# Local attention of a head pair: from three blocks of three query tiles to one block of nine

## Chip, cores and metric

One core of one Trainium2 chip runs the whole program. The metric is the device time of one execution in microseconds (us); for the kernel before it is 1076.56 us, the median of three runs (1076.06 to 1077.1).

## What is computed

An attention with 2 batches, 8 heads, 576 positions and a head width of 64 feeds a layer with 8 experts and then a dense layer with a softplus. The change touches the attention alone, which adds two parts: a coarse attention over means of 4 positions, and a local one in which a position sees only positions less than 4 away. All is fp32.

```python
def _attn_ref(q, k, v):
    ...
    out_d = sm_attn(q_d, k_d, v_d)              # means of 4 positions
    out_up = np.repeat(out_d, factor, axis=2)
    mask = np.abs(pos[:, None] - pos[None, :]) < factor
    scores = scale * np.matmul(q, k.transpose(0, 1, 3, 2))
    scores = np.where(mask, scores, -1000000000.0)
    scores = scores - np.max(scores, axis=-1, keepdims=True)
    attn = np.exp(scores)
    attn = attn / (np.sum(attn, axis=-1, keepdims=True) + 1e-09)
    out_local = np.matmul(attn, v)
    return (out_up + out_local).astype(np.float32)
```

## The kernel before

**Units.** The attention is cut into eight units, one for each pair of heads: units 0 to 3 are batch 0, units 4 to 7 batch 1. A unit has 9 query tiles of 64 positions. A local query tile meets a window of 72 keys. `load` fetches q, k and v of a unit; there is one buffer for q and k (`qk`), so the load of a unit waits until the unit before has been transposed. `setup(g)` transposes three tiles into the bank `tb`, from which VectorE (DVE) sums groups of 4 (L535), ScalarE (ACT) scales the keys (L546), and both copy the queries into `fine`, in which the columns of one head are zero in the rows of the other (L547, L548).

**Blocks.** A unit then goes through four blocks: `c`, the coarse part, and 0, 1 and 2, three query tiles each, with both heads side by side in the 128 rows. Each block has three steps. `scores` forms the products into one PSUM bank `sc` (for a local block one product lays the mask there at L572 and three add the scores at L578), takes the maximum of each row (DVE, L585), three exponentials with their sums (ACT, L590), the reciprocal and the product with it (DVE, L591 to L593). `turn` transposes the result (L615) and ACT copies it (L616). `values` multiplies by v (L637), and DVE adds the coarse part into `xf` (L652).

**Order.** The loop at L1039 walks 32 blocks and issues `scores` of block n, `turn` of block n-2 and `values` of block n-3; `setup` of the next unit stands beside blocks 1 and 2. A scheduler then orders the instructions of each engine, and each engine works through its list in that order. `stir` (L481) issues products that nothing reads, in units 0 to 3 only.

**Beside the attention.** Once the four units of batch 0 are done, `operands` turns their output into the split operands of the expert products (subtractions at L437, rounding on ACT at L439, remainders on DVE at L441). The first four steps of the expert products (L841, L929) run among the units of batch 1. When the last unit is done, the operands of the other tokens are formed, and the rest of the program follows in an order fixed by a planner; its instructions are not touched by the change.

Of the kernel before, what the change touches and what calls it, by code (L numbers as in the profile page):

```python
# [9 lines left out]
F32 = mybir.dt.float32  # L10
F32R = mybir.dt.float32r
U32 = mybir.dt.uint32
BF16 = mybir.dt.bfloat16
# [7 lines left out]
def attention_moe_mlp(ctx: ExitStack, tc: tile.TileContext, q, k, v, w_gate, w1, w2, w_in, w_out, out):  # L21
# [10 lines left out]
    NQ = S // QT  # L32
    NB = 3
# [30 lines left out]
    ps = ctx.enter_context(tc.tile_pool(name="ps", bufs=1, space=PSUM))  # L64

    def bank(tag, name):
# [394 lines left out]
    mask = ap.tile([P, NB + 2, KW], BF16, bufs=1, name="mask")  # L461
    nc.gpsimd.memset(mask, 0.0)
    for t0, t1, off in ((0, 1, 0), (1, NB + 1, R), (NB + 1, NB + 2, 2 * R)):

        for hh in range(2):
            part = mask[hh * QT : (hh + 1) * QT, t0:t1, :]
            for sign in (1, -1):
                nc.gpsimd.affine_select(
                    out=part, in_=part, compare_op=ALU.is_gt, fill=NEG,
                    base=R + sign * off, pattern=[[0, t1 - t0], [-sign, KW]], channel_multiplier=sign,  # L470
                )
    rest = const.tile([P, KD, LEFT], F32, name="rest")

    fine = [ap.tile([P, NB, 2, QT], F32, bufs=1, name=f"fine{g}") for g in range(NB)]
    flat = [ap.tile([P, NB, 2, CT], F32, bufs=1, name=f"flat{i}") for i in range(2)]
    for x in fine + flat:
        nc.gpsimd.memset(x, 0.0)
# [8 lines left out]
    class Unit:  # L486
# [9 lines left out]
        def bank(self, name, kind):  # L496
            return bank(("m", "at", "y")[kind] if self.b == 0 else "at", name)
# [23 lines left out]
        def setup(self, g):  # L521

            if g == 0:
                self.kT = ap.tile([P, NQ, QT], F32, tag="kT", name="kT")
# [4 lines left out]
            for j in range(NB):  # L529
# [4 lines left out]
            tbv = tb.rearrange("x (t w p) -> x t w p", t=NB, w=2)  # L534
# [23 lines left out]
        def scores(self, blk):  # L558

            sc = self.bank("sc", 0)  # L560
            stir(sc, 1 if self.n < 4 else 0)
            if blk == "c":
                rows, w = 2 * CT, SD
                for i in range(NB):
                    nc.tensor.matmul(
                        sc[:rows, i * w : (i + 1) * w], self.flat[:, i].rearrange("x h q -> x (h q)"),
# [616 lines left out]
```

## Time and profile before

| what | us |
|---|---|
| three runs | 1076.06, 1076.56, 1077.1 |
| median | 1076.56 |
| span of the profiled execution | 1075.4 |
| last value products of the attention | 140.8 to 141.7 |

The span goes from the first to the last instruction. The profiled execution has no time listed beside its span; the median of the runs lies 1.16 us above it. In the views, PE is TensorE's product stream and PEld its weight load, DVE is VectorE, ACT ScalarE, POOL GpSimd, SP the engine that issues the transfers. A product in fp32 leaves two records, a transpose one. PEclk is the clock granted to TensorE as a share of 2.4 GHz; 0.50 is 1.2 GHz.

### The profile page before, as it was taken

What the parts mean: (1) busy time and instruction counts of PE and PEld (TensorE: products, weight loads), DVE (VectorE), ACT (ScalarE), POOL (GpSimd) and SP (SyncE); (2) the same over time, 40 slices, a digit from 0 to 9 for tenths busy, and PEclk for the clock granted to TensorE, in tenths of its full rate; (3) what the DMA queues carried; (4) which work ended last, traced back from release to release, by engine and by line L of the source; (5) the groups of instructions that cost most, each with busy time, mean ns of one, the idle gap of its engine ahead of it and who ended that gap; (6) DMA issues with size and microseconds to landing.
All of it is one profiled execution on the core that took longest, in us unless ns stands there. A gap on an engine that the chain in (4) does not pass through costs nothing.

```text
span 1075.4 us, 17729 instructions
## 1 busy us (share of the span) xinstructions
PE 1052.5 (98%) x6426; PEld 933.1 (87%) x6426; DVE 697.6 (65%) x1430; ACT 567.0 (53%) x1475; POOL 555.4 (52%) x575
## 2 busy tenths in 40 slices
PE   7989999999999999999999999999999999999998
PEld 4778888898989999898989989899998999788987
DVE  4797655776556566665656566565664678776765
ACT  3777634444444444454544444444454667676663
POOL 4556614477566566655566565664575412232221
PEclk8989989999999999999999999999999999999999
DMA  7654301222433334243333333343324373253112
GB/s 156 128 137 92 92 1 40 59 87 78 138 108 98 113 93 127 92 130 108 118 122 95 93 95 112 98 124 116 119 93 144 137 297 145 108 220 143 69 40 89
DMA packets 133495, 119.69 MB, mean 111 GB/s; under 512 B 35744, under 2 KB 111776, under 8 KB 133408
## 3 DMA queue, kind: packets, MB, share of 16 engines
q1 hardware_dynamic: 133408, 118.56, 36.1%
q8 instruction: 50, 0.82, 0.3%
q14 instruction: 37, 0.30, 0.1%
HBM read 93.11 MB, written 25.43 MB: 110 GB/s over the span
## 4 chain that ended last, share of the span: by engine, by line
PE 81%; DVE 10%; ACT 5%; POOL 1%; issue 1%; DMA 1%; SPq 1%; ACTq 0%; DVEq 0%
PE yps L929 40%; PE m L841 36%; DVE xl L441 2%; DVE ab L808 2%; POOL ab L805 1%; DVE ab L801 1%; ACT one L803 1%; PE sc L578 1%; DVE one L799 1%; ACT sc L590 1%; DVE c L860 1%; PE pv L637 1%; DVE hl L812 1%; PE tp L615 0%; DVE hl L780 0%
## 5 line engine op out<-in xcount | busy, mean ns | idle before, releaser
L841 PE MATMUL m<-xh,w1h 128*128 128x320 f32 (+1 forms) x1120 | 334.7, 299 | 2.8 <-DVE hl L780 1.6
L841 PE MATMUL m<-xl,w1h 128*128 128x320 f32 (+1 forms) x1120 | 333.3, 298 | 0.3 <-DVE xl L441 0.2
L841 PE MATMUL m<-xh,w1l 128*128 128x320 f32 (+1 forms) x1120 | 333.3, 298 | 0.0
L841 PEld LDWEIGHTS m<-xh,w1h 128*128 128x128 f32 x1120 | 213.1, 190 | 19.8 <-ACT t L853 2.8
L841 PEld LDWEIGHTS m<-xl,w1h 128*128 128x128 f32 x1120 | 213.1, 190 | 13.2 <-DVE xl L441 0.7
L841 PEld LDWEIGHTS m<-xh,w1l 128*128 128x128 f32 x1120 | 213.0, 190 | 0.4 <-POOL sums L244 0.2
L929 PE MATMUL yps<-w2h,hh 128*128 128x512 f32 x502 | 199.0, 396 | 2.2 <-ACT hh L810 2.2
L929 PE MATMUL yps<-w2l,hh 128*128 128x512 f32 x502 | 198.1, 395 | 0.0
L929 PE MATMUL yps<-w2h,hl 128*128 128x512 f32 x502 | 195.9, 390 | 0.0
L929 PE MATMUL yps<-w2h,h 128*128 128x512 f32 x436 | 153.0, 392 | 0.1
L295 POOL TENSOR_TENSOR w1l<-sums,w1h 128x512 fp32r<-128x512 f32 x72 | 99.2, 1389 | 88.7 <-ACT w1h L293 78.0
L860 DVE TENSOR_TENSOR c<-m,t 128x256 f32<-128x256 f32 (+1 forms) x160 | 72.7, 455 | 110.3 <-PE m L841 64.8
L316 POOL TENSOR_TENSOR w2l<-raw,w2h 128x512 fp32r<-128x512 f32 x72 | 98.4, 1385 | 59.8 <-ACT w2h L314 59.4
L805 POOL TENSOR_TENSOR ab<-one,ab 128x320 f32<-128x320 f32 (+1 forms) x64 | 54.6, 855 | 143.3 <-ACT one L803 143.3
L778 ACT ACTIVATE hh<-c 128x256 fp32r<-128x256 f32 (+1 forms) x138 | 61.0, 445 | 126.4 <-DVE c L860 126.2
L959 DVE SCALAR_TENSOR_TENSOR acc<-yps,pr,acc 128x512 f32<-128x512 f32 x117 | 87.3, 746 | 55.4 <-PE yps L929 54.7
L780 DVE SCALAR_TENSOR_TENSOR hl<-c,hh 128x256 fp32r<-128x256 f32 (+1 forms) x138 | 94.3, 687 | 33.0 <-ACT hh L778 31.4
L929 PEld LDWEIGHTS yps<-w2h,hl 128*128 128x128 f32 x502 | 94.3, 188 | 22.0 <-DVE hl L812 0.2
L929 PEld LDWEIGHTS yps<-w2h,hh 128*128 128x128 f32 x502 | 94.7, 189 | 15.2 <-ACT hh L810 2.6
L853 ACT COPY t<-m 128x256 f32<-128x256 f32 (+1 forms) x160 | 63.4, 398 | 78.4 <-PE m L841 78.2
L929 PEld LDWEIGHTS yps<-w2l,hh 128*128 128x128 f32 x502 | 94.8, 189 | 10.8
L929 PEld LDWEIGHTS yps<-w2h,h 128*128 128x128 f32 x436 | 82.0, 188 | 15.2 <-ACT h L810 0.3
(140 smaller groups left out, 1660.4 us busy)
## 6 DMA issues: line engine op xcount, KB each, us to landing
raw<-in_moe_w SPq DMA_DIRECT2D x72, 256.0 KB
raw<-in_moe_w SPq DMA_DIRECT2D x36, 512.0 KB
w1h<-s_in SPq DMA_DIRECT2D x10, 896.0 KB
w1l<-s_in SPq DMA_DIRECT2D x10, 896.0 KB
raw<-in_moe_w_in SPq DMA_DIRECT2D x32, 256.0 KB
raw<-in_moe_w_out SPq DMA_DIRECT2D x16, 512.0 KB
w2l<-s_out SPq DMA_DIRECT2D x10, 512.0 KB
w2h<-s_out SPq DMA_DIRECT2D x10, 512.0 KB
```

The lines of the kernel that those rows point to most:

```text
L295: behind(chain, nc.gpsimd.tensor_tensor(lo[:, part], sums, hi[:, part].bitcast(F32), op=ALU.subtract))
L316: behind(chain, nc.gpsimd.tensor_tensor(lo[:, i], raw[:, i], hi[:, i].bitcast(F32), op=ALU.subtract))
L441: nc.vector.tensor_tensor(xl[s][:, i, kk], src, xh[s][:, i, kk].bitcast(F32), op=ALU.subtract)
L778: nc.scalar.activation(hh, c, AF.Relu)
L780: nc.vector.scalar_tensor_tensor(out=hl, in0=c, scalar=0.0, in1=hh.bitcast(F32), op0=ALU.max, op1=ALU.subtract)
L805: nc.gpsimd.tensor_tensor(ab, one, ab, op=ALU.subtract)
L808: nc.vector.scalar_tensor_tensor(out=ab, in0=c, scalar=0.0, in1=ab, op0=ALU.max, op1=ALU.add)
L841: nc.tensor.matmul(b[:, :h], x[:, i, kk, :], y[s][:, i, kk, :], start=(not more and n == 0), stop=(n == 5), skip_group_check=more,)
L853: nc.scalar.copy(t, b[:, :h])
L860: nc.vector.tensor_tensor(c, b[:, :h], t, op=ALU.add)
L929: nc.tensor.matmul(y, a[:, f, tok], b[:, f, :], start=(start and m == 0), stop=(stop and m == 5))
L959: nc.vector.scalar_tensor_tensor(out=acc[t], in0=y, scalar=pr[:, t, e : e + 1], in1=acc[t], op0=ALU.mult, op1=ALU.add,)
```

## The change

The three local blocks of a unit become one block of nine tiles. Its scores lie in two PSUM banks (`two`), one for each head, five windows of 72 columns in each, with even tiles in rows 0 to 63 and odd tiles in rows 64 to 127. A product now has 64 rows of contraction and 64 of output, so `fine` and its zeros go; the keys are not scaled, ACT's exponential scales instead. DVE subtracts the maximum, one exponential on ACT covers all 720 columns, and DVE sums the rows. PSUM is dealt out anew: in batch 1 the single banks of the attention come from two buffers (`one`) where there were four (`at`). A copy of `rest` moves from DVE to ACT, and the values of a unit go through two banks (5 and 4 tiles) where there were three.

```diff
     def bank(tag, name):
...
-        return ps.tile([P, 512], F32, tag=tag, bufs=4 if tag == "at" else 1, name=name)
+        if tag in ("at", "one"):
+            return four[0].tile([P, 512], F32, tag=tag, bufs=4 if tag == "at" else 2, name=name)
+        return ps.tile([P, 512], F32, tag=tag, name=name)
...
-            return bank(("m", "at", "y")[kind] if self.b == 0 else "at", name)
+            return bank(("m", "one", "y")[kind] if self.b == 0 else "one", name)
...
+            nc.scalar.copy(
+                self.qkT[:, :, tiles].rearrange("x w t p -> x t w p"), tb.rearrange("x (t w p) -> x t w p", t=NB, w=2)
+            )
...
-            nc.scalar.mul(self.kT[:, tiles], tbv[:, :, 1], SCALE)
-            nc.vector.tensor_copy(fine[g][:D, :, 0], tbv[:D, :, 0])
-            nc.scalar.copy(fine[g][D:, :, 1], tbv[D:, :, 0])
...
+        def local(self):
+
+            sc = four[0].tile([P, 2, 512], F32, tag="two", name="sc2")
+            stir(sc[:, 0], 1 if self.n < 4 else 0)
+            kT = self.qkT[:, 1].rearrange("x t q -> x (t q)")
+            for hh in range(2):
+                nc.tensor.matmul(
+                    sc[:, hh, : NP2 * KW], identb, mask.rearrange("p t w -> p (t w)"),
+                    start=True, stop=False, skip_group_check=True,
+                )
+            for t in range(NQ):
+                w0 = min(max(t * QT - R, 0), S - KW)
+                for hh in range(2):
+                    half = slice(hh * D, (hh + 1) * D)
+                    nc.tensor.matmul(
+                        sc[t % 2 * QT : (t % 2 + 1) * QT, hh, t // 2 * KW : (t // 2 + 1) * KW],
+                        self.qkT[half, 0, t], kT[half, w0 : w0 + KW],
+                        start=False, stop=(t >= NQ - 2), skip_group_check=True,
+                    )
+            scv = sc[:, :, : NP2 * KW].rearrange("p h (i s) -> p h i s", i=NP2)
+            small = ap.tile([P, 3, 2, NP2, 1], F32, tag="smalls", name="smalls")
+            top, total, rs = [small[:, i] for i in range(3)]
+            ex = ap.tile([P, 2, NP2, KW], F32, tag="exl", bufs=1, name="exl")
+            whole = [P, 2, NP2, KW]
+            nc.vector.tensor_reduce(top, scv, axis=AX.X, op=ALU.max)
+            nc.vector.tensor_tensor(scv, scv, top.to_broadcast(whole), op=ALU.subtract)
+            nc.scalar.activation(scv, scv, AF.Exp, scale=SCALE)
+            nc.vector.tensor_reduce(total, scv, axis=AX.X, op=ALU.add)
+            nc.vector.tensor_scalar(rs, total, EPS, None, op0=ALU.add)
+            nc.vector.reciprocal(rs, rs)
+            nc.vector.tensor_tensor(ex, scv, rs.to_broadcast(whole), op=ALU.mult)
+            self.state["l"] = ex
...
-                et = ap.tile([KW, NB * P], F32, tag="et", name="et")
-                tp = self.bank("tp", 1)
-                stir(tp, 1 if self.n < 4 else 0)
-                for i in range(NB):
-                    nc.tensor.transpose(tp[:KW, i * P : (i + 1) * P], ex[:, i, :], ident)
-                nc.scalar.copy(et, tp[:KW, : NB * P])
+                et = ap.tile([KW, 2, S], F32, tag="et", bufs=1, name="et")
+                full = NQ // 2
+                for hh in range(2):
+                    tp = self.bank("tp", 0)
+                    stir(tp, 1 if self.n < 4 else 0)
+                    for i in range(full):
+                        nc.tensor.transpose(tp[:KW, i * P : (i + 1) * P], ex[:, hh, i], ident)
+                    nc.scalar.copy(et[:, hh, : full * P], tp[:KW, : full * P])
...
-    blocks = ["c", 0, 1, 2]
+    blocks = ["c", "l", None, None]
```

DVE's list for unit 2, before: L585 is a block's maximum, L591 to L593 its end, L535 a setup sum of unit 3, L652 an addition of unit 1 into `xf`.

```order
L585 TENSOR_REDUCE small<-sc 96x3
L585 TENSOR_REDUCE small<-sc 128x3
L652 TENSOR_TENSOR xf<-pv,xc 128x192
L585 TENSOR_REDUCE small<-sc 128x3
L535 TENSOR_REDUCE qkd<-tb 128x96 x2
L591 TENSOR_SCALAR small<-sc 96x3
L652 TENSOR_TENSOR xf<-pv,xc 128x192
L592 RECIPROCAL small<-small 96x3
L591 TENSOR_SCALAR small<-sc 128x3
L593 TENSOR_TENSOR ex<-sc,small 96x432
```

The same place with the change: L580 and L586 to L588 are the coarse block, L615, L616, L618 to L621 the local one, L537 the setup sums, L687 the additions into `xf`.

```order
L615 TENSOR_REDUCE smalls<-sc_527 128x10
L586 TENSOR_SCALAR small<-sc 96x3
L537 TENSOR_REDUCE qkd<-tb 128x96 x2
L616 TENSOR_TENSOR sc_527<-sc_527,smalls 128x2x360
L587 RECIPROCAL small<-small 96x3
L687 TENSOR_TENSOR xf<-pv,xc 128x256
L537 TENSOR_REDUCE qkd<-tb 128x96
L588 TENSOR_TENSOR exc<-sc,small 96x432
L694 COPY rest<-xf 128x64
L618 TENSOR_REDUCE smalls<-sc_527 128x10
L546 TENSOR_SCALAR flat_141<-qkd 64x3x48 x2
L619 TENSOR_SCALAR smalls<-smalls 128x10
```

L620 and L621 follow. Before, three maxima and three ends of blocks stand interleaved; now one chain of maximum, subtraction, sum and product runs through the list.

PE's list from the end of unit 1 into unit 2, before: a transpose group (L615), the mask and scores of one local block (L572, L578), the coarse scores (L565), value products of the block before (L637).

```order
L615 MATMUL tp<-ident,ex 72x128 x3
L481 LDWEIGHTS identb
L481 MATMUL sc<-identb 128x512
L572 LDWEIGHTS identb
L572 MATMUL sc<-mask,identb 128x216
L578 MATMUL sc<-kT,fine_149 128x72 x3
L565 MATMUL sc<-qkd,flat_152 96x144 x3
L637 MATMUL pv<-et,vw 64x64 x6
L615 MATMUL tp<-ident,ex 72x128 x3
```

With the change, from the transposes of unit 1's block (L645) to the last local scores of unit 2 (L605), L597 being the mask, L660 and L573 the coarse values and scores, L676 the value products:

```order
L645 MATMUL tp<-ident,exl 72x128 x8
L484 LDWEIGHTS identb
L484 MATMUL sc_527<-identb 128x512
...
L649 MATMUL tp<-ident,exl 72x64 x2
L660 MATMUL pv<-etc,vs 64x144 x3
L605 MATMUL sc_527<-qkT 64x72 x3
L484 LDWEIGHTS identb
L484 MATMUL sc<-identb 128x512
L573 MATMUL sc<-qkd,flat_140 96x144 x3
L605 MATMUL sc_527<-qkT 64x72 x8
L676 MATMUL pv<-et,vw 64x64 x10
L605 MATMUL sc_527<-qkT 64x72 x4
```

All scores of a unit now stand behind the transposes of the block before and partly behind its value products, where before a third of them did.

## Rows read from the trace of the kernel before

**Rows 1.** The page's first part: busy time of each engine over the span.

```profile
PE 1052.5 (98%) x6426; PEld 933.1 (87%) x6426; DVE 697.6 (65%) x1430; ACT 567.0 (53%) x1475; POOL 555.4 (52%) x575
```

**Rows 2.** Busy time by stretch: PE, PEld, DVE, ACT, POOL, granted clock, DMA.

```profile
28.00:58.00 30.00, 25.42 (x268) 19.74 (x263) 23.59 (x81) 23.51 (x107) 16.27 (x20) 1.00 0.61 134
58.00:68.00 10.00, 10.00 (x45) 7.82 (x43) 9.85 (x18) 6.33 (x21) 8.39 (x10) 0.50 0.42 104
68.00:77.00 9.00, 8.56 (x90) 7.27 (x90) 7.99 (x28) 8.19 (x35) 3.91 (x4) 0.99 0.55 155
77.00:142.00 65.00, 64.28 (x560) 55.28 (x560) 43.74 (x127) 43.20 (x161) 36.31 (x39) 1.00 0.36 83
```

**Rows 3.** PE in order of time: start, length; coarse scores of units 1 to 4, two more.

```profile
26.82 0.92 PE L565 MATMUL sc<-qkd,flat 128*96 128x144 f32 x6
...
38.57 0.92 PE L565 MATMUL sc<-qkd,flat 128*96 128x144 f32 x6
...
49.45 0.92 PE L565 MATMUL sc<-qkd,flat 128*96 128x144 f32 x6
...
56.95 0.69 PE L605 MATMUL tp<-ident,ex 96*72 96x96 f32 x6 [2.16 <-DVE ex L593]
...
64.06 1.64 PE L565 MATMUL sc<-qkd,flat 128*96 128x144 f32 x6
...
140.83 0.92 PE L637 MATMUL pv<-et,vw 72*64 72x64 f32 x24
```

**Rows 4.** Groups by shape, 8 to 72 us: count | busy, mean ns of one.

```profile
L590 ACT ACTIVATE sc<-sc,small 128x72 f32<-128x72 f32 x39 | 11.6, 311 | 3.1 <-DVE small L585 2.9
L535 DVE TENSOR_REDUCE qkd<-tb 128x96 f32<-128x384 f32 x16 | 8.4, 548 | 6.7 <-PE tb L530 6.6
L590 ACT ACTIVATION_READ_ACCUMULATOR sc<-sc,small 128x1 f32 x39 | 6.3, 161 | 0.0
L590 ACT ACTIVATE sc<-sc,small 96x144 f32<-96x144 f32 x15 | 5.4, 360 | 8.6 <-DVE small L585 8.5
L585 DVE TENSOR_REDUCE small<-sc 128x3 f32<-128x216 f32 x14 | 5.2, 374 | 3.6 <-PE sc L578 3.6
L547 DVE COPY fine<-tb 64x192 f32<-64x192 f32 x15 | 4.9, 339 | 0.2
L593 DVE TENSOR_TENSOR ex<-sc,small 128x216 f32<-128x216 f32 x12 | 4.5, 376 | 0.2
L652 DVE TENSOR_TENSOR xf<-pv,xc 128x192 f32<-128x192 f32 x11 | 3.8, 346 | 0.8 <-PE pv L637 0.5 <-ACT sc L590 0.2
L648 DVE COPY xf<-rest 128x64 f32<-128x64 f32 x2 | 3.3, 1706 | 0.0
L585 DVE TENSOR_REDUCE small<-sc 96x3 f32<-96x432 f32 x5 | 3.0, 601 | 7.5 <-PE sc L565 7.5
L591 DVE TENSOR_SCALAR small<-sc 128x3 f32<-128x3 f32 x13 | 1.8, 149 | 0.6 <-ACT sc L590 0.4
```

**Rows 5.** The chain that ended last, in pieces: start, length, what.

```profile
25.57 4.59 DMA qk<-in_k
...
82.28 0.47 PE yps L929 x2
82.75 0.50 PE pv L637 x12
83.25 0.43 PE yps L929
83.79 0.64 PE sc L578 x6
...
110.45 2.75 PE yps L929 x12
...
137.71 0.45 PE tp L615 x3
...
142.78 7.10 DVE xl L441 x10
```

More of the change, by code (lines that the diff above doesn't have):

```diff
@@ L32, in attention_moe_mlp @@
     NQ = S // QT
+    NP2 = (NQ + 1) // 2
     NB = 3
@@ L64, in attention_moe_mlp @@
     ps = ctx.enter_context(tc.tile_pool(name="ps", bufs=1, space=PSUM))
+    psa = tc.tile_pool(name="psa", bufs=1, space=PSUM)
+    four = [psa.__enter__()]
     def bank(tag, name):
@@ L459, in attention_moe_mlp @@
     nc.vector.tensor_copy(identb, ident)
-    mask = ap.tile([P, NB + 2, KW], BF16, bufs=1, name="mask")
+    mask = ap.tile([P, NP2, KW], BF16, bufs=1, name="mask")
     nc.gpsimd.memset(mask, 0.0)
[L463 to L471, printed above, removed]
+    for odd, t0, t1, off in ((0, 0, 1, 0), (0, 1, NP2 - 1, R), (0, NP2 - 1, NP2, 2 * R), (1, 0, NP2, R)):
+        part = mask[odd * QT : (odd + 1) * QT, t0:t1, :]
+        for sign in (1, -1):
+            nc.gpsimd.affine_select(
+                out=part, in_=part, compare_op=ALU.is_gt, fill=NEG / SCALE,
+                base=R + sign * off, pattern=[[0, t1 - t0], [-sign, KW]], channel_multiplier=sign,
+            )
     rest = const.tile([P, KD, LEFT], F32, name="rest")
-    fine = [ap.tile([P, NB, 2, QT], F32, bufs=1, name=f"fine{g}") for g in range(NB)]
     flat = [ap.tile([P, NB, 2, CT], F32, bufs=1, name=f"flat{i}") for i in range(2)]
-    for x in fine + flat:
+    for x in flat:
         nc.gpsimd.memset(x, 0.0)
@@ L643, in values @@
             kk = u % 2
[L644 to L658 removed]
+            for t0, t1 in ((0, NP2), (NP2, NQ)):
+                pv = self.bank("pv", 2)
+                for t in range(t0, t1):
+                    for hh in range(2):
+                        nc.tensor.matmul(
+                            pv[hh * D : (hh + 1) * D, (t - t0) * QT : (t - t0 + 1) * QT], self.vw[:, t, hh],
+                            et[:, hh, t * QT : (t + 1) * QT], start=True, stop=True,
+                        )
+                if t0 == 0:
+                    if u < 2:
+                        self.pairs[s, kk] = pair("xf")
+                    if s:
+                        nc.scalar.copy(self.pairs[s, kk][:, u // 2, :LEFT], rest[:, u])
+                xf = self.pairs[s, kk][:, u // 2]
+                s0, w = t0 * QT, (t1 - t0) * QT
+                nc.vector.tensor_tensor(
+                    xf[:, base + s0 : base + s0 + w].rearrange("p (g r) -> p g r", r=R),
+                    pv[:, :w].rearrange("p (g r) -> p g r", r=R),
+                    self.xc[:, s0 // R : (s0 + w) // R].unsqueeze(2).to_broadcast([P, w // R, R]),
+                    op=ALU.add,
+                )
+            if s == 0:
                 nc.vector.tensor_copy(rest[:, u], xf[:, S - LEFT : S])
@@ L1042, in attention_moe_mlp @@
             i, j = divmod(n, len(blocks))
-            x.scores(blk)
+            if blk:
+                x.scores(blk)
             if waiting:
@@ L1069, in attention_moe_mlp @@
     at.__exit__(None, None, None)
+    psa.__exit__(None, None, None)
+    four[0] = ctx.enter_context(tc.tile_pool(name="psb", bufs=1, space=PSUM))
     operand_tiles(ctx.enter_context(tc.tile_pool(name="xp1", bufs=1)), 1)
```

68 lines of the change are left out of this document (21 added, 47 removed).

## Prediction

> **What bounds the kernel now.** I read the page first: TensorE (PE) is busy for 98% of the span, which says little, since its records overlap [rows 1]. The table by stretches shows where others set the pace [rows 2]. From 77 to 142 us PE is busy for 64.28 of 65 us at the full clock: expert products fill every gap of the attention, and PE is the bound. Before 77 us it is not. From 28 to 58 us VectorE (DVE) and ScalarE (ACT) are both near 79%; from 58 to 77 DVE is busy for 17.8 of 19 us. The list of PE in order of time gives the rhythm: the coarse scores of units 1 to 4 stand at 26.82, 38.57, 49.45 and 64.06, so a unit takes 11.75, 10.88 and 14.61 us [rows 3]. It also shows what a sparse PE costs: at 56.95 PE had waited 2.16 us for a product on DVE, and from 58 to 68 us the granted clock is 0.50, that is 1.2 GHz [rows 2, 3]; coarse scores then take 1.64 us instead of 0.92. The attention's last value products end near 141.7 [rows 3]; a chain of remainders on DVE follows (7.10 us from 142.78 [rows 5]) that the change doesn't touch. What the change does to the time is therefore how far that end moves.
>
> **The parts, priced.** ACT: nine exponentials of 72 columns with nine reads of the sum cost 9 x (0.311 + 0.161) = 4.2 us per unit [rows 4]. From 72 to 144 columns the price rises by 0.049, so one of 720 costs about 0.360 + 8 x 0.049 = 0.75: ACT gains 3.5 us per unit. DVE: 216 columns cost 0.374 and 432 cost 0.601, so a reduction of 720 costs 0.90; I price the subtraction and the last product alike, since 216 columns cost 0.376 there [rows 4]. Four passes of 0.90 and two short ones of 0.15 make 3.9 us, against three blocks of 0.374 + 0.376 + 2 x 0.15, 3.2 us. Gone are three copies into `fine` (3 x 0.339); the additions into `xf` go from 3 x 0.346 to about 0.9, as 320 columns cost 0.48 and 256 cost 0.41. So DVE gains 0.5 us per unit. The two copies of `rest` that took 1.7 us each leave DVE [rows 4]. A subtraction that writes PSUM has no row; from the product of the same length to twice that is the bound, and I take the product. PE: nine score products had 18 records of 0.107, 1.9 us [rows 5]. Now 36 records have 64 weight columns; the nearest row is the value products, 0.042 a record at 64 columns, so 0.047 at 72: 1.7 us. From 0.025, if two halves run side by side, to 0.107, the bound is 0.9 to 3.9. The mask goes from three products of 216 columns to two of 360, with a 512-column product at 0.23 [rows 5], no difference. The gain of PE is about 0.2 us per unit; the two `stir` groups it also loses were filling idle time.
>
> **What the merging adds.** Work falls, but the order now has a loop. In PE's new list all local scores of unit 2 stand behind the transposes of unit 1's block, and the last four behind ten of its value products. From the product that ends unit 1's block PE has: 8 transposes (1.2, at 0.45 for three), two `stir` (0.46), masks (0.32), coarse scores (0.92) and three coarse value products (0.6 by the same row), the 18 products (1.7), ten value products (20 records, 0.83): 6.0 us. Only then can DVE take the maximum. Its list to the end of the block is: maximum 0.90, two setup sums 1.10, subtraction 0.90, `xf` 0.41, a setup sum 0.55, the coarse product 0.60, the sum 0.90, two `flat` writes 0.6 (half of 0.339 each is the least, 0.339 the most), the product 0.90, five short ones 0.75: 7.6 us. The exponential (0.75) hides behind the setup sums. While PE works its 6.0 us, DVE has the coarse maximum, one `xf` and remainders, so it idles for 3 to 4 of them. The period is 13.6 us where it was 11.75 and 10.88; ACT's 3.5 us lie beside it and buy nothing. The first unit is earlier: its scores no longer wait for `fine`, and I put the coarse scores of unit 1 at 26.4, as now. From there to those of unit 4 are three periods, less 2.5 us since unit 4's stand ahead of the transposes: 38.3 against 37.2, **+1.1**. Should `qk` be late (4.59 us from issue to landing [rows 5]), its wait stands ahead of eight value products and of DVE's setup sums; up to 1.5 us more, kept for the range.
>
> From unit 4's coarse scores to the point where PE is full took 13 us. DVE's list there now holds unit 4's local chain (3.9) and coarse block (1.5), a setup (2.2), `xf` (0.9) and thirteen remainders and subtractions of 256 columns (0.42 each by the price above, 5.5), 14.0 us without a wait: **+1.5** with half a microsecond of wait. In the PE-full stretch three units save 0.2 each: **-0.6**. The last unit's transposes, copies and value products now pass through two banks and stand behind the last expert products, where only 0.92 us of value products stood [rows 3]; three waits for copies of about 0.4: **+1.3**. At the full clock the sum is +3.3.
>
> **The clock.** In each period PE now has 7.6 us with only 2 to 3 us of work, three times the wait that came before the fall at 58. If it falls in a period, PE's 6.0 us grow. Bounds for units 1 to 4 are 0 and 4 x 6.0 = 24; part of the present 10 us at 0.50 hides behind DVE, and I take an eighth, **+3**.
>
> The sum stands against the profiled execution: 1075.4 + 6.3 = 1081.7 of span, and 1.16 to the median, **1082.9 us**. A measurement of this kernel tells about 0.2% (2.2 us) from no change.
>
> **Rivals.**
> (a) *The queues stay filled and the work counts.* If DVE finds enough of the next unit's setup to do in PE's 6.0 us, the period follows DVE's load. For it: DVE and ACT are at 79% from 28 to 58, and the 14.6 us of unit 3 hold ACT's weight casts. Against: one buffer for `ex`, `et` and the double bank. Three periods lose 0.6 each, unit 3 gains 2 more from ACT, DVE loses 2 x 1.7 of `rest`, and 1.5 us are given back: -5.7, **1071**. It decides if the period stays below 11 us.
> (b) *Even.* A period near 12.5 and an end without waits for banks: within 2.2 us of now, as 65 us of full PE follow either way.
> (c) *The 64-row products cost what the padded ones did.* 36 records at 0.107 add 2.2 us per unit to three periods and to three units where PE is full: 13 more on the sum at full clock, **1093**. Against: value products on 64 columns follow expert products and are followed by them without a gap in the chain (82.28 + 0.47, 82.75 + 0.50, 83.25) [rows 5]. The Trainium skill, TensorEngine Tiling (Array Packing), section Key Properties, says for this: "Mode switching requires drain", so every change between shapes of array would empty it, and the new list mixes shapes more. The chain's gapless pieces don't agree for 64-column products; no row shows 64-row ones.
> (d) *The clock stays at 0.50 through the early units*: +24 in place of +3, **1104**.
>
> **How the numbers follow.** Forecast 0.42, (a) 0.28, (b) 0.13, (c) 0.10, (d) 0.07. Slower is 0.59, same 0.13, faster 0.28. The range runs from (a), with a little room, to (c): 1070 to 1094, leaving out (d) and about half of (a). The forecast's own range is 1079 to 1090.
>
> **What would show it.** Right: coarse scores of units 2 and 3 some 13 to 14 us apart; DVE idle before the new maximum until the local scores; more stretches at 0.50 before 70 us; ACT's busy time some 28 us lower in all without effect; PE full from about 80 us; the last `xf` 3 to 8 us later than 142. Step by step wrong: a period of 11 us or less (the loop is not there), 0.107 a record in the new scores (my price for PE), gaps on PE behind 80 us that end with an ACT copy (two banks cost more than 1.3). If the end of the attention moves and the total doesn't, the fixed part behind it has slack that I don't see.

## The result and the profile after the change

The changed kernel takes **1086.56 us** (median of 5 runs, 1085.31 to 1088.03) where the kernel before, on the same chip, takes 1076.56 (5 runs, 1072.27 to 1080.95). The ratio is 1.0093, 95% interval 1.0068 to 1.0118: slower by 10 us. The profiled execution of the changed kernel took 1086.56 us with a span of 1084.8.

| profiled execution | before | after |
|---|---|---|
| span, us | 1075.4 | 1084.8 |
| PE idle in the span (span less busy) | 22.9 | 35.4 |
| of it in the first 170 us | 14.6 | 27.8 |
| mean granted clock | 0.987 | 0.981 |
| ACT busy | 567.0 | 550.6 |
| coarse scores of unit 4 at | 64.06 | 69.98 |
| last `xf` of the attention at | 141.54 | 154.73 |

The page's first part, which answers to [rows 1]:

```profile
PE 1049.4 (97%) x6558; PEld 923.4 (85%) x6558; DVE 700.3 (65%) x1346; ACT 550.6 (51%) x1319; POOL 552.8 (51%) x568
```

PE is busy for 3.1 us less although the run is 9.4 us longer, so PE's idle time grew by 12.5 us. The table says where: by 13.2 us in the first 170 us, and by nothing behind them. Up to unit 4's coarse scores PE idles for 19.4 us where it was 12.6, from there to the last `xf` for 7.3 where it was 1.2: about half of the growth lies in each. Busy time by stretch, in the columns of [rows 2]:

```profile
28.00:58.00 30.00, 23.84 (x242) 15.81 (x246) 20.57 (x43) 13.03 (x37) 10.19 (x16) 0.74 0.55 108
58.00:68.00 10.00, 7.39 (x96) 5.66 (x89) 8.00 (x15) 7.17 (x21) 9.23 (x9) 0.84 0.48 119
68.00:77.00 9.00, 8.70 (x92) 6.48 (x91) 6.76 (x14) 6.55 (x21) 6.23 (x9) 0.71 0.93 195
77.00:142.00 65.00, 58.35 (x542) 48.48 (x537) 47.30 (x96) 36.47 (x99) 38.90 (x42) 1.00 0.36 96
```

Two things differ. From 28 to 58 us no engine is near its limit any more: DVE fell from 23.59 to 20.57 and ACT from 23.51 to 13.03, and yet the units follow each other more slowly. And from 77 to 142 us, where PE had been the bound with 64.28 of 65 us, it is now busy for 58.35. The list of PE in order of time, as in [rows 3]:

```profile
19.63 1.51 PE L533 MATMUL tb<-ident,qk 128*128 128x128 f32 x6 [4.55 <-DMA qk<-in_k]
...
29.02 0.98 PE L573 MATMUL sc<-qkd,flat 128*96 128x144 f32 x6
...
32.37 1.51 PE L533 MATMUL tb<-ident,qk 128*128 128x128 f32 x6 [1.64 <-DMA qk<-in_k]
...
37.11 1.17 PE L633 MATMUL tp<-ident,exc 96*72 96x96 f32 x6 [1.33 <-DVE exc L588]
...
44.23 0.90 PE L573 MATMUL sc<-qkd,flat 128*96 128x144 f32 x6
...
50.92 0.69 PE L633 MATMUL tp<-ident,exc 96*72 96x96 f32 x6 [1.59 <-DVE exc L588]
...
59.00 1.17 PE L573 MATMUL sc<-qkd,flat 128*96 128x144 f32 x6
...
65.94 0.56 PE L533 MATMUL tb<-ident,qk 128*128 128x128 f32 x3 [2.50 <-ACT qkT L541]
...
69.98 1.76 PE L573 MATMUL sc<-qkd,flat 128*96 128x144 f32 x6
```

The coarse scores of units 1 to 4 stand 15.21, 14.77 and 10.98 us apart, where it was 11.75, 10.88 and 14.61; in each period PE waits: for the load of q and k, for `exc` on DVE, or until ACT has copied q and k out of a bank. In the stretch that had been full, the waits of PE from 77 to 142 us (engine and line that waited, releaser, total, times, longest) are:

```profile
PE tb L533 <- ACT qkT L541: 1.6, 1, 1.6
PE yps L964 <- ACT hh L813: 1.6, 1, 1.6
PE tp L633 <- ACT qkT L541: 1.1, 2, 0.7
PE yps L964 <- DVE acc L986: 0.9, 1, 0.9
PE tb L533 <- DVE xf L687: 0.6, 1, 0.6
```

The kernel before has one wait of 0.7 there. Read the first, third and fifth row by what the waiting instruction reads: the transposes of L533 read only `qk` and `ident`, those of L633 `exc` and `ident`. Neither reads `qkT` or `xf`. So I read these as waits for the bank that `qkT` and `xf` had to be copied out of: 3.3 of the 6.65 us that PE idles there. The 2.50 us at 65.94 in the list above are of the same kind. The second row is another matter. The chain of waits shows what is behind it:

```profile
130.68 1.41 POOL w2l L321
...
132.10 3.33 DMA raw<-in_moe_w
...
135.46 1.14 ACT w2h L319 x2
136.59 0.29 ACT hh L813
...
136.93 0.73 PE yps L964 x2
```

A weight load waits for its one buffer until POOL is done with the load before; the cast of those weights on ACT waits for the load, and `hh`, which PE needs now, stands behind the cast in ACT's queue.

Last, an order on SP that I had not looked at: before, q and k of unit 1 were issued at 8.92 us; now two weight loads (three transfers) stand ahead of them.

```profile
8.85 1.27 SPq L270 DMA_DIRECT2D raw<-in_moe_w  x2
10.16 0.64 SPq L315 DMA_DIRECT2D raw<-in_moe_w  x1
10.93 1.29 SPq L509 DMA_DIRECT2D qk<-in_q  x2
12.26 2.53 SPq L509 DMA_DIRECT2D qk<-in_k  x2
```

### The profile page after: what moved, and what is told of

The parts are those of the page before. It is cut to its first block, busy times and chain, and to the rows that moved or that the text cites. A ratio compares the mean times of both kernels' runs of the same rounds, so it can differ in the third digit from the quotient of the medians.

```text
span 1084.8 us, 17719 instructions
## 1 busy us (share of the span) xinstructions
PE 1049.4 (97%) x6558; PEld 923.4 (85%) x6558; DVE 700.3 (65%) x1346; ACT 550.6 (51%) x1319; POOL 552.8 (51%) x568
## 4 chain that ended last, share of the span: by engine, by line
PE 77%; DVE 10%; ACT 4%; POOL 3%; DMA 3%; SPq 1%; issue 1%; ACTq 0%; POOLq 0%; DVEq 0%
PE yps L964 39%; PE m L876 34%; DMA raw<-in_moe_w 2%; DVE ab L843 2%; POOL ab L840 1%; DVE xl L446 1%; DVE ab L836 1%; ACT one L838 1%; POOL sums L249 1%; DMA qk<-in_k 1%; DVE one L834 1%; PE tp L645 1%; DVE xf L442 1%; SPq L509 1%; DVE hl L847 1%
## 5 line engine op out<-in xcount | busy, mean ns | idle before, releaser
L964 PEld LDWEIGHTS yps<-w2h,h 128*128 128x128 f32 x436 | 82.2, 189 | 15.1 <-ACT h L845 0.3
```

Source lines behind the costliest of these rows:

```text
L964: nc.tensor.matmul(y, a[:, f, tok], b[:, f, :], start=(start and m == 0), stop=(stop and m == 5))
```

## Experiments

Five theories, most of which can hold together. **S**: the swap on SP makes the early units late. **L**: the merged block is a loop in which PE and DVE take turns, and the clock falls. **B**: the double bank leaves two single banks for the second batch, too few to keep PE fed. (The setup transposes of the first batch have two buffers in the changed kernel too, where they had a share of four.) **W**: the weight loads and their sums come late and block ACT. **P**: the parts by themselves (64-row products, one exponential per block) cost or gain. One more came up on the way, **O**: any edit reorders the queues, and the new order itself costs.

The lists of all engines in the attention come out of a scheduler, and each of these edits moved them in 30 to 60 places. No run below is therefore a pure change of one thing. Ratios are to the kernel before on the same chip in the same session. "Idle" is PE's idle time in the first 170 us of the profiled execution (170 less PE's busy time in that window).

| kernel | banks of the second batch | ratio, 95% interval | median, us | idle, us | unit 4's coarse scores | last `xf` |
|---|---|---|---|---|---|---|
| before | 4 single | 1 | 1076.56 | 14.6 | 64.06 | 141.54 |
| after | double + 2 single | 1.0093, 1.0068 to 1.0118 | 1086.56 | 27.8 | 69.98 | 154.73 |
| a_sp | double + 2 single | 1.0072, 1.0053 to 1.0091 | 1085.26 | 25.4 | 63.90 | 152.32 |
| a_head | double + 2 single | 1.0102, 1.0084 to 1.0121 | 1087.93 | 27.6 | 62.80 | 157.71 |
| a_stir | double + 2 single | 1.0077, 1.0061 to 1.0093 | 1085.30 | 21.6 | 66.68 | 153.51 |
| c_sp | 4 single | 1.0049, 1.0031 to 1.0068 | 1081.93 | 17.0 | 73.51 | 152.90 |
| c_stir | 4 single | 1.0071, 1.0055 to 1.0087 | 1083.97 | 14.4 | 69.14 | 143.28 |
| b_bank2 | 2 single | 1.0260, 1.0242 to 1.0278 | 1104.88 | 24.8 | 68.69 | 170.38 |
| b_exp | 4 single | 1.0044, 1.0024 to 1.0064 | 1081.82 | 18.9 | 69.69 | 155.72 |
| b_rows | 4 single | 1.0030, 1.0011 to 1.0049 | 1079.44 | 18.2 | 66.89 | 148.65 |
| n_swap | 4 single | 1.0024, 1.0009 to 1.0038 | 1079.93 | 20.9 | 65.76 | 146.29 |
| n_head | 4 single | 1.0029, 1.0016 to 1.0042 | 1080.74 | 15.9 | 62.52 | 145.11 |
| m_rows | 4 single | 0.9981, 0.9967 to 0.9996 | 1075.67 | 15.1 | 62.09 | 136.94 |
| m_pair | double + 2 single | 1.0156, 1.0142 to 1.0170 | 1092.81 | 24.3 | 71.65 | 161.89 |

The profiled executions of c_sp, b_exp and b_rows took 1088.45, 1088.39 and 1085.60 us, each the longest of its kernel, so their last three columns are worse than their medians.

The last column is a delay only in part. An order also decides how many expert products stand ahead of the last `xf`: of the second expert product (`yps`) it is 84 records before, 96 after, 60 in m_rows and 96 in m_pair, and one follows the other by 0.23 us. I set beside it what PE idles from unit 4's coarse scores to the last `xf`: 1.2 us before, 7.3 after.

### a_sp: the swap on SP undone

```diff
+            if f in AHEAD:
+                tc.add_manual_dep(
+                    ins.ins, landing[AHEAD[f]].ins.name,
+                    mybir.DependencyInfo(mybir.DependencyClass.Sync, mybir.DependencyReason.DATA),
+                )
...
+    AHEAD = {0: 1, 4: 7}
```

`AHEAD` names the step whose first weight loads wait, and the unit whose q and k they wait for. It has a second entry: step 4 waits for unit 7, so the run touches the second half too.

> The changed kernel, with one thing added: the first weight loads of the expert products wait on the q and k load of unit 1, so that this load stands ahead of them on SP, as it did before the change (there at 8.92 us, in the changed kernel at 10.93 behind four weight loads). Theory S (part of the loss is this swap on SP, which I hadn't foreseen: PE then waits 4.55 and 1.64 us for q and k): the coarse scores of unit 4 come back from 69.98 to about 66, and the time falls from 1086.6 to about 1083. Theory L (the loop of the merged block, in which PE and DVE take turns and the granted clock falls to 0.50, sets the periods of the units anyway): the waits for q and k go, waits for DVE take their place, unit 4 stays within 1 us of 69.98 and the time within 1 us of 1086.6. The list of PE shifts in some 30 places with any such edit, which alone may move the time by about 1 us.

Measured: unit 4's coarse scores come at 63.90, 6.1 us earlier than after the change and where they were before it. That fits theory S, but it doesn't show it: a_head below leaves the weight loads ahead (q and k of unit 1 at 10.71 us), and its unit 4 comes at 62.80. The total falls by only 1.3 us by the medians, 2.3 by the ratios, with overlapping intervals. From unit 4's coarse scores to the last `xf` it is now 88.4 us, where it was 77.5 before and 84.8 after: what was won up to unit 4 is lost behind it. PE does not idle more there (5.5 us, after 7.3), but the granted clock is 0.92 where it was 0.98. And up to unit 4 PE still idles for 18.8 us. So the swap is not what costs the time, and there is loss to explain in both halves.

### b_bank2: the kernel before, with two banks for the second batch

```diff
-            return bank(("m", "at", "y")[kind] if self.b == 0 else "at", name)
+            return bank(("m", "o", "y")[kind] if self.b == 0 else "o0", name)
```

`o` is `o0` and `o1` in turn, two buffers each; the first batch still has all four, the second only `o0`.

> The kernel before, with two PSUM banks in place of four for the attention of the second batch (units 4 to 7), as many as the changed kernel leaves for it beside the double bank. Theory B (fewer banks is what costs the second half of the attention, where PE of the changed kernel is busy for 58.35 us of 77 to 142 in place of 64.28): PE falls below 61 us in that stretch, the last xf comes 4 us or more later than 141.8, and the time is about 1081. Theory W (the second half is lost to weight loads and sums that were delayed by the first half, not to banks): PE stays at 63 us or more there and the time is 1077, within 1 us.

Measured: slower by 2.6%, 28 us, far over the 5 that I expected of theory B. Busy time by stretch, and the longest waits of PE from 77 to 165 us:

```profile
77.00:142.00 65.00, 56.68 (x415) 48.69 (x415) 40.68 (x108) 38.89 (x133) 29.81 (x34) 0.89 0.27 63
```

```profile
PE sc L578 <- DVE xf L658: 3.0, 3, 2.0
PE pv L643 <- ACT et L622: 1.6, 3, 0.7
```

L578 is here the mask product that opens the scores of a block. It reads the mask and `identb`, not `xf`: PE waits until DVE has read `xf`'s input out of its bank. With nothing of the change in it, taking two banks away turns a PE that was full into one that waits, at a clock of 0.89: from unit 4's coarse scores to the last `xf` PE idles for 12.0 us, where it was 1.2, and up to them for 12.8, much as before. In this order of blocks two banks are too few. It does not yet say that this is what costs in the changed kernel, which asks for banks less often.

### b_exp and b_rows: one part each

```diff
+                nc.vector.tensor_tensor(scv, scv, off.to_broadcast([rows, NB, w]), op=ALU.subtract)
+                nc.scalar.activation(scv, scv, AF.Exp)
+                nc.vector.tensor_reduce(total, scv, axis=AX.X, op=ALU.add)
```

> The kernel before, where each block of three query tiles takes one exponential of 216 columns with a subtraction ahead of it and a sum behind it on DVE, in place of three exponentials of 72 columns with the sums read by ACT. Per unit ACT loses about 2.9 us and DVE gains 2.2. If the time goes by DVE in the stretches where it is busy for 17.8 of 19 us (units 3 and 4), this part of the change alone makes it slower: about 1079. If the three short ACT instructions and their reads of the sum are what the chain of a block waits for, it is faster: about 1074. If neither, 1076.6 within 1 us.

Measured: 1.0044, about 5 us slower, on the side of "DVE sets the time there". But see the controls below: some 3 us of it may be the order.

```diff
-                        sc[:, i * w : (i + 1) * w], fine[blk][:, i].rearrange("x h q -> x (h q)"),
...
+                    for hh in range(2):
+                        half = slice(hh * D, (hh + 1) * D)
...
+                            sc[half, i * w : (i + 1) * w], self.qT[half, t],
```

> The kernel before, with the 64-row products of the change alone: q is kept unpadded by ACT (no fine, no zeros, one copy less on DVE per group of three tiles), each local score is two products of 64 rows that write their halves of the same bank; blocks of three tiles, nine exponentials of 72 columns and four banks stay. Theory P (this part is good by itself, and the loss is in how the block is merged): the 64-row products run two at a time, some 0.03 us a record as in the changed kernel, so PE loses over 1 us of work per unit, and DVE 1 us per unit where it is the bound: about 1072. Rival (the products of different array shapes disturb each other, or the copies lost were no bound): 1076.6 within 1 us, or slower. The orders of all engines shift in some 50 places, which alone may move the time by 2 us or so either way.

Measured: 1.0030, some 3 us slower; the 1072 of theory P did not come. The products themselves are quicker. At the full clock the mask product and the scores of a group of three tiles are

```profile
87.91 0.27 PE L571 MATMUL sc<-mask,identb 128*128 128x216 bf16 x1
88.11 0.59 PE L579 MATMUL sc<-kT,qT 64*64 64x72 f32 x12
```

where the padded scores took 0.80 for 6 records and here it is 0.59 for 12; three groups per unit make 1.8 us in place of 2.4. So neither part brings a gain by itself in this kernel, and whether they cost one can't be told from what follows.

### n_swap and n_head: two controls that change no work

```diff
-            nc.scalar.mul(self.kT[:, tiles], tbv[:, :, 1], SCALE)
             nc.vector.tensor_copy(fine[g][:D, :, 0], tbv[:D, :, 0])
             nc.scalar.copy(fine[g][D:, :, 1], tbv[D:, :, 0])
+            nc.scalar.mul(self.kT[:, tiles], tbv[:, :, 1], SCALE)
```

> A control: the kernel before, with one line moved, the scaled copy of k on ACT behind the two copies of q into fine rather than ahead of them. The same instructions with the same sizes; but the order of all engines in the attention shifts in about 60 places, as many as with any of the edits so far. Theory O (part of every loss measured so far is the new order itself: the order of the kernel before happens to be a good one, and any edit leaves it): the control loses 2 to 5 us, 1079 to 1081. Theory P' (the losses of 3 to 5 us of the single parts are those parts' own): the control is at 1076.5 within 1.5 us.

```diff
-                for hh in range(2):
+                for hh in (1, 0):
```

> A second control: the kernel before, with the two heads' value products of a query tile in the other order. Same instructions, same sizes, no engine's load moves; some 30 places of the orders shift. Theory O: 1078 to 1081. Theory P': 1076.5 within 1.5 us.

Measured: 1.0024 and 1.0029, both slower, by 2.6 and 3.1 us, with intervals that leave out 1. Theory O holds for these two: an edit that changes no instruction's size or engine costs this kernel some 3 us. That is as much as the whole loss of b_rows, and all but some 2 us of b_exp's. As much of the changed kernel's 10 us may belong to no part of the change; what its own order costs isn't measured. Over half of the controls' loss may go with the clock: their runs were at 0.50 for 33.4 and 34.5 us in the median, the kernel before for 27.9, which at 0.28 us each (see a_stir) is an estimated 1.5 and 1.8 us.

### a_head and a_stir: the chain on DVE, and the clock

```diff
-            nc.vector.tensor_reduce(top, scv, axis=AX.X, op=ALU.max)
+            for hh in range(2):
+                nc.vector.tensor_reduce(top[:, hh], scv[:, hh], axis=AX.X, op=ALU.max)
...
```

> The changed kernel, with the seven passes over its double bank taken head by head (360 columns each) on DVE and ACT; banks, buffers and products as they are. Theory L (what costs is that DVE's chain of a block is serial with PE: four passes of 0.9 us one behind the other and an exponential of 0.75 between them): the second head's passes cover the exponential of the first, the chain is some 1.3 us shorter, periods of the early units fall by 1 us each, and the time falls to 1084. Theory B (the double bank has one buffer and two single banks carry all else, so PE can't run ahead however the passes are cut): within 1 us of 1086.6, or slower by the fixed costs of four more passes, 0.15 us each.

Measured: 1.0102, no faster than the change. Cutting the passes by head, with the banks as they are, brings the early units forward (unit 4 at 62.80) and the end back (last `xf` 157.71). PE idles less up to unit 4 (14.3 us) and more behind it (12.1). A shorter chain on DVE does not bring the time back, as theory B expected.

```diff
+            if self.n < 4:
+                for _ in range(2):
+                    stir(self.bank("sx", 0), 5)
```

> The changed kernel, with ten more idle products of 512 columns (2.3 us) behind the local scores of each of units 0 to 3, where PE waits for DVE's chain: no work, only to keep PE busy. Within the runs of the kernel before, one microsecond more at a granted clock of 0.50 goes with 0.29 us more of time; the changed kernel has some 41 us at 0.50 against 27. Theory C (the clock carries about 4 us of the 10 lost): the time at 0.50 falls below 25 us and the total to about 1082. Rival (the time at 0.50 only shows where PE waits, and costs nothing of its own): the total stays at 1086.6 or rises, by up to 9 us if the idle products stand in front of work that was ready.

A run's time at 0.50 follows from its span and mean clock, 2 x (1 - clock) x span. Measured: it falls from 41 us (median of the runs) to 30, not below 25, and the total by 1.3 us, to 1.0077, with overlapping intervals. Within the kernel before (35 runs of two sessions) a microsecond at 0.50 goes with 0.28 us of time, so 11 of them should give back 3. Whether the idle products take part of that again isn't shown. Theory C is neither shown nor ruled out; by that slope the 13 us more at 0.50 that the changed kernel has (41 against 28) are an estimated 4 us of its loss. Filling PE's waits with empty work buys little.

### c_sp and c_stir: one block per head, in single banks

```diff
-            sc = four[0].tile([P, 2, 512], F32, tag="two", name="sc2")
+            sc = self.bank("sc2", 0)
...
-            ex = ap.tile([P, 2, NP2, KW], F32, tag="exl", bufs=1, name="exl")
+            ex = ap.tile([P, NP2, KW], F32, tag="exl", bufs=2, name="exl")
...
-    blocks = ["c", "l", None, None]
+    blocks = ["c", 0, 1, None]
```

The dependency of a_sp is in it too.

> The changed kernel with one local block per head in place of one per pair: a single bank each, one exponential of 360 columns, two buffers of its result, so that PE works on the scores of one head while DVE works on the other, four banks for the attention of the second batch as before the change, and the q and k load of unit 1 ahead of the weight loads as in the run above. Theory L (the loop of the double bank): unit periods fall to 11 or 12 us, unit 4's coarse scores come at 64 or earlier, and the time is 1076 or less, if 64-row products and long exponentials are good in themselves as low as 1072. Theory that the long passes on DVE cost what they cost in any order: about 1082. Theory B and W as above: without the double bank the second half also comes back, PE at 62 us or more from 77 to 142.

Measured: 1.0049, about 5 us slower than before and by the ratios 2 to 6 faster than the four kernels with the double bank above, though the intervals of a_sp and a_stir overlap with its own. Even in its longest execution, the profiled one, PE is full again where it was full before:

```profile
77.00:142.00 65.00, 64.25 (x599) 54.11 (x598) 48.29 (x120) 39.16 (x116) 36.23 (x41) 0.91 0.34 88
```

The 1076 of theory L did not come, nor unit 4 at 64 or earlier; the other half of theory B did: here, without the double bank, PE idles for 1.6 us from unit 4's coarse scores to the last `xf`. a_head against c_sp is the comparison: passes by head in both, but in c_sp each head's block has its own bank and buffer, and four single banks stand where there were two. (The dependency on SP differs too.)

For c_stir, to this:

```diff
+            if self.n < 4:
+                stir(self.bank("sx", 0), 5)
```

> The kernel with one local block per head (1081.9 us), with five more idle products behind the local scores of each head of units 0 to 3. Its profiled run was at 0.50 for 59 us and took 1088, its others were at 0.50 for 24 to 46 us and took 1079 to 1085, some 0.24 us for each microsecond. Theory C: it holds the clock up, 20 us or less at 0.50, and the time is 1078, which with four banks in the second half is even with the kernel before. Rival (the extra products cost their 9 us where PE has no slack): 1085 or more.

Measured: 1.0071, some 2 us slower than c_sp. The idle products cost, and the clock gave nothing back: c_sp's runs were at 0.50 for 32 us in the median, and these too. PE is busy for 61.33 us of 77 to 142 here, with four single banks: an order can empty that stretch without any lack of banks.

### m_rows and m_pair: the merged block only where PE is full

```diff
+            if self.n >= 4 and blk != "c":
+                return self.local(blk)
```

`local` is that of c_sp: one head, one bank, one exponential of 360 columns. Units 0 to 3 have the blocks of b_rows. So that all fits, q has one buffer per group of three tiles and `et` one per unit.

> A mixture: 64-row products in all units; blocks of three tiles with nine exponentials in units 0 to 3, where PE waits for chains, and one block per head with one exponential of 360 columns, in single banks, in units 4 to 7, where PE is full; four banks for the attention of the second batch. If the merged form is worth having where PE is full and harmful only where it waits, the second half saves about 1 us of PE per unit and this is the fastest of all: 1073 to 1076. If the loss lies in the order alone (theory O), 1078 to 1082.

Measured: **1075.67 us, 0.9981 (0.9967 to 0.9996)**: faster than the kernel before, by 0.2%, and 4 to 5 us better than the controls, whose orders are as new as its own. It is the one faster kernel of twelve, and its gain of 2 us is no more than what a new order by itself moved in the controls; so how much of it is the merged form isn't shown.

```profile
77.00:142.00 65.00, 63.80 (x619) 53.48 (x618) 47.81 (x119) 41.07 (x122) 38.93 (x42) 1.00 0.31 83
```

PE is as full as before, the score products of units 4 to 7 take 2 x 0.84 us per unit where the padded ones took 2.4, and the last `xf` comes at 136.94 instead of 141.54. That it comes earlier is no gain by itself: 24 fewer records of `yps` stand ahead of it, 5.5 us at 0.23 each.

```diff
-            return bank(("m", "at", "y")[kind] if self.b == 0 else "at", name)
+            return bank(("m", "one", "y")[kind] if self.b == 0 else "one", name)
...
+            sc = four[0].tile([P, 2, 512], F32, tag="two", name="sc2")
```

> The mixture that took 1075.7 us, with the block of units 4 to 7 as in the change: both heads in one double bank with one buffer, two single banks for all other work of the second batch, one exponential of 720 columns (the last product is taken head by head, so that it fits the buffers). Units 0 to 3 keep blocks of three tiles. Theory B (the double bank costs in the second half, where two single banks are too few to keep PE fed): PE is busy for 61 us or less of 77 to 142, the attention's last xf comes after 145 (137.4 in the mixture), and the time is 1080 to 1085. Theory L alone (the loss of the change was made in units 0 to 3, before PE is full): the second half stays full and the time is 1077 or less. An order that shifts in some 50 places may add 2 to 3 us by itself, as the two controls show, so between 1077 and 1080 it stays open.

Measured: 1.0156, by the medians 17 us slower than m_rows, more than expected. The longest wait is ahead of unit 4's coarse scores: from 66.7 to 71.6 us PE waits 4.91 us, because an ACT copy stands behind a weight cast that waits for sums on POOL.

```profile
71.65 1.75 PE L659 MATMUL sc<-qkd,flat 128*96 128x144 f32 x6 [4.91 <-ACT et L717]
```

These scores read `qkd` and `flat`, not `et`: PE waits for one of the two single banks, the one that `et` is copied out of. That this copy comes so late is an accident of the order. Behind the wait the granted clock is 0.56 up to unit 5's coarse scores at 92.84.

From unit 5's coarse scores to the last `xf` it takes 69.1 us (92.84 to 161.89), with single banks 57.4 (79.56 to 136.94). That looks like 12 us for the double bank in the second half, but most of it is work that changed places: 36 more records of `yps` stand in the stretch, 8.3 us at 0.23 each. PE idles there for 3.3 us against 0.8. From 77 to 142 us PE is busy for 61.62 us at a clock of 0.90, just above the 61 that theory B allowed. Up to unit 4's coarse scores PE idles for 18.8 us against 11.9, the 4.91 among them, though units 0 to 3 have the same blocks; but their transposes have two buffers here and four in m_rows. So theory L alone (1077 or less) is out: the double bank with two single ones costs much in this order, without a merged block in the first half. That it costs it by a second half that is never full, as theory B says, isn't shown by this run: the larger part is one wait for a bank and the low clock behind it.

Over all kernels, PE idles from unit 4's coarse scores to the last `xf` for 4.9 to 12.1 us in the six with a double bank or two banks, and for 1.2 to 5.5 in the eight with four single banks. b_bank2 and c_sp are the clearest on either side.

**What stays open.** Theory W was seen at work (the cast ahead of `hh`; in the wait of 4.91 us it and the lack of a bank meet), but no run moved the weight loads of the second half by themselves. Whether they are late because the attention is, or the other way round, isn't settled. Nor is how the 10 us divide: the controls put an order alone at 2.6 to 3.1; c_sp against the changed kernel puts the double bank with its loop, and the swap on SP, at 4.7 by the ratios; the swap alone (a_sp) is within the noise. No run has the block of a pair with four single banks beside it, so the loop and the lack of banks are not told apart.

## Why the prediction was right, and where its steps failed

Forecast 1082.9, measured 1086.56: slower, as forecast, inside the range. By its steps:

**The prices on DVE and ACT: right for one instruction.** The groups by shape of the changed kernel:

```profile
L616 DVE TENSOR_TENSOR sc<-sc,smalls 128x720 f32<-128x720 f32 x8 | 7.3, 912 | 0.2
...
L615 DVE TENSOR_REDUCE smalls<-sc 128x10 f32<-128x720 f32 x8 | 7.2, 903 | 3.8 <-PE sc L605 3.8
...
L687 DVE TENSOR_TENSOR xf<-pv,xc 128x320 f32<-128x320 f32 x8 | 3.9, 483 | 3.8 <-PE pv L676 3.8
...
L619 DVE TENSOR_SCALAR smalls<-smalls 128x10 f32<-128x10 f32 x8 | 1.9, 237 | 0.1
```

```profile
L617 ACT ACTIVATE sc<-sc 128x720 f32<-128x720 f32 x8 | 6.0, 756 | 3.7 <-DVE sc L616 3.4
```

0.90 was forecast for each long pass, the subtraction in PSUM among them, 0.48 for `xf`, 0.75 for the exponential. Only the two short ones take 0.24 and 0.21, not 0.15. The sums of them came out too large: ACT's busy time fell by 16.4 us, not by 28. Its instructions overlap, so that nine times 0.311 + 0.161 is more than the time they hold ACT: before, an exponential starts at 85.79, its read at 85.99 and the next exponential at 86.18, 0.39 us for both in place of 0.47.

**The score products: too dear.** 1.7 us per unit was taken (0.047 a record, bounds 0.025 to 0.107). The records:

```profile
84.92 0.47 PE L597 MATMUL sc<-mask,identb 128*128 128x360 bf16 x2
85.32 0.59 PE L605 MATMUL sc<-qkT 64*64 64x72 f32 x20
...
86.88 0.48 PE L605 MATMUL sc<-qkT 64*64 64x72 f32 x16
...
102.21 0.35 PE L605 MATMUL sc<-qkT 64*64 64x72 f32 x8
```

36 records take 0.59 + 0.48 = 1.07 us. From 8 to 20 records 0.24 us are added, 0.02 each: below my lower bound. That rules out **rival (c)**: these products cost less than half of the padded ones' 2.4 us. Standing between products of other shapes has a price, but a small one: from the start of the mask product of 216 columns to the first padded score it is 0.11 us (83.52 to 83.63 before), to the first 64-row score 0.20 (87.91 to 88.11 in b_rows). In the kernel before:

```profile
82.12 0.40 PE L929 MATMUL yps<-w2h,hh 128*128 128x512 f32 x1
82.35 0.40 PE L929 MATMUL yps<-w2l,hh 128*128 128x512 f32 x1
82.68 0.57 PE L637 MATMUL pv<-et,vw 72*64 72x64 f32 x12
...
83.52 0.27 PE L572 MATMUL sc<-mask,identb 128*128 128x216 bf16 x1
83.63 0.80 PE L578 MATMUL sc<-kT,fine 128*128 128x72 f32 x6
```

The rule that the Trainium skill states under TensorEngine Tiling (Array Packing), Key Properties, that a switch of mode drains the array, would give such a price, and it fits these two numbers, at some 0.1 us a change; that it is the drain, no run shows by itself. The value products showed it already: two `yps` start 0.23 apart and the value products 0.33 behind them. The chain in [rows 5], whose pieces lie end to end, doesn't show that. What the cheaper scores gave back can't be seen in the total.

**Unit 1's coarse scores at 26.4: wrong, 29.02.** ("As now" was a slip: it is 26.82 in [rows 3].) I moved the work on PE, DVE and ACT and left SP's list where it was. The case of a late `qk` was named, with up to 1.5 us kept for the range; it was behind two weight loads, and PE waited 4.55 us for it at 19.63, three times what was kept.

**The period of 13.6 us: right in kind, too short.** 15.21, 14.77 and 10.98 came, 40.96 us in all where 38.3 was forecast and 37.24 had been. The waits named are there (DVE's chain, `qk`), and one that wasn't: 2.50 us for a bank. DVE does wait for PE, 5.10 and 1.92 us in the two periods, but for the coarse scores; ahead of the local maximum, where the prediction put the wait, it is 1.4 us in all from 29 to 70. That the period decides the time was wrong: a_sp and a_head bring unit 4's coarse scores forward by 6 and 7 us, and the total didn't follow (1.3 us less, 1.4 more).

**The end of the attention: this is the step that failed.** "Unit-4 stretch +1.5, PE-full stretch -0.6, tail with two banks +1.3", together +2.2. From unit 4's coarse scores to the last `xf` it is 84.8 us in place of 77.5: +7.3, and PE's idle time in it is 6.1 of that. PE was not full from 80 us, as the prediction had said: it is busy for 58.35 of 65. I put the price of two banks on the last unit alone, three waits of 0.4. By the waits listed above it is paid from unit 4 on, 3.3 us between 77 and 142; most of the rest is waits on the expert products' side (`hh`, `acc` and two smaller ones, 3.1 us), for which the sum had no term. b_bank2 shows what two banks can come to in another order: 28 us.

**The clock, +3: not contradicted.** 13 us more at 0.50, at 0.28 us each, are an estimated 4 us. No run shows the term by itself, and the eighth that I took was a choice; that the two agree is in part luck. **Rival (d)** supposed that units 1 to 4 stay at 0.50 throughout; the granted clock there was 0.71 to 0.84.

**The end of the attention as the measure: wrong.** The last `xf` is 13.2 us later, where 3 to 8 were named, and the span 9.4 longer. The prediction's words for that were slack in the fixed part behind. The trace shows something else for most of the 3.8 us: 12 records of `yps`, 2.8 us at 0.23 each, stand ahead of the last `xf` now and stood behind it before. Over the whole run PE does less work: busy time is 3.1 us less although the part of it at 0.50 grew from 25.6 to 33.6 us, which at the full clock is a further 4 less, some 7 us in all.

So that the total lies within 4 us of the forecast is partly luck: the end moved by 13.2 us where the sum had 6.3, and 3.8 us of that did not reach the span.

**Rival (a)**, 1071 us, asked for periods below 11 us and queues that stay filled. In the changed kernel neither came. m_rows, which keeps the merged form out of the stretch where PE waits, and the double bank out of all, gains 2 us; whether that is a part of the gain that (a) had in mind isn't shown.

## What to carry to other kernels

A block that is merged across heads saves instructions, and asks for a wide buffer with few copies of it; what it costs is the work that could run ahead while that buffer is held. So count the banks that the other steps are left with, in every stretch where they share them, and above all in the stretch that is now full. Merge, if at all, where the engine that gains is the bound, and leave the banks alone: the one kernel here that wasn't slower did so, though it won no more than an order is worth. And don't take the last instruction of a part for its end, where other work can change places with it: count what stands ahead of it. And before a difference of some tenths of a percent is put down to an edit, time a control that changes the order of the queues and nothing else.

## What the runs showed that I had not expected

- **64-row products differ in cost between three forms.** With the two heads in turn and a bank each, 12 more records behind the first 8 took 0.24 us. With both heads in turn in one bank (b_rows), 12 records take 0.59 us, where the changed kernel takes 0.47 for 12. With one head after the other (c_sp, m_rows), 18 take 0.84, where 20 in turn take 0.59. Bank and half of the columns weren't varied one at a time:

```profile
95.38 0.84 PE L614 MATMUL sc<-qkT 64*64 64x72 f32 x18
```

- **An order that changes no work cost 2.6 and 3.1 us** (0.24% and 0.29%) in two controls of this kernel.
- **The time at 0.50 differs between executions of one and the same kernel**, and the time goes with it: among 35 runs of the kernel before it was 17 to 39 us, with 0.28 us of time for each of them.
